# Causal scores in three blocks per head, spread over both column halves, no idle matmuls between the first round's digits, and one product more per digit in the second round

## The chip, the cores and the metric

One core of a Trainium2 chip. The metric is the time of one execution on the device in microseconds (us). The fast executions of one kernel in a group of runs agree within some 1.5%, so ratios are given with a 95% interval, from fast executions alone. Executions count as "slow" over 1.5% above the fastest of the same kernel. All others are undisturbed ("fast"). Engines are named as in the profile: PE (TensorE, matmul), PEld (its weight loads), DVE (VectorE), ACT (ScalarE), POOL (GpSimd), SP (SyncE, which issues most loads).

## The reference

Two parts, one after the other, with q, k, v and f_logit of 4 x 8 heads x 768 x 48 in fp32:

```python
f = sigmoid(f_logit)
for t in range(768):                                # gated linear attention, per head
    state = f[t][:, None] * state + outer(k[t], v[t])
    y[t] = q[t] @ state
x = y as (3072 tokens, 384)
logits = x @ w_gate                                 # 8 experts
# all 3072*8 logits in falling order; a token takes an expert that has fewer than 384 tokens
out[tokens of e] = relu(x[tokens of e] @ w1[e]) @ w2[e]      # 384 -> 1024 -> 384
```

## The kernel before

The attention runs in 24 chunks of 128 positions (6 for each of the 4 batches, all 8 heads at once). Each loop step works on several chunks at different stages: the pair of a part and a number is the part and how many steps the chunk lags. In the traces an engine's instructions run in the order of the program (ACT in one step: "high" at 93.84 us, the copies of x at 94.24, of q at 95.18, the decays from 96.86), so a part's place in this list is its place in an engine's queue.

```python
BANKS = {"bank": 6, "sum": 2}            # PSUM: six banks used in turn, two for the output sums

def scores(G):                            # A = k q^T, two keys halves j, two head parities par
    A = [ps("A") for _ in range(2)]
    ...
    for hp in range(HP):                  # HP = 4 head pairs
        for j in range(2):
            for par in range(2):
                ...                       # rows: the partitions of head 2*hp + par
                nc.tensor.matmul(out=A[par][HC*j:HC*j+HC, 128*hp:128*hp+128],     # HC = 64
                                 lhsT=G["kT"][rows, hp, HC*j:HC*j+HC],
                                 rhs=G["qT"][rows, hp, :], start=True, stop=True)
    for par in range(2):                  # the causal mask is applied in the copy out of PSUM
        nc.vector.copy_predicated(am[:, par], mask..., A[par]...)

FIRST = ((decayed, 2), (q_columns, 2), (k_columns, 2), (transposed, 5), (sums, 1))
FILLING = FIRST + ((x_copy, 5), (factors, 1), (k_copy, 2), (added, 2), (values, 4), (halves, 1),
                   (gate, 5), ..., (split, 0), (clamp, -1), (queries, 4), (scores, 3))
```

In the profile's lines A is the scores, T the transposes of q and k, X the transposes of x and the gate products, L the gate's cumulated sums, dS (part `added`) the state product, Y the outputs (`values`, then `queries`). ACT copies T to qT, Y to x, and prepares the decays.

After it come eight rounds of expert assignment. A round finds a threshold by digits (compare on DVE, count on PE), lists the tokens of an expert, gathers their rows by an indirect DMA from POOL, transposes them (Xe, copied to xeT by ACT) and runs the two expert products H and O. The products of one expert are queued one by one in `pe_work` and dealt out between the digits of the next round, so that PE has something to do:

```python
pace = {0: None, 1: (2, 1)}               # second round: 2 products before a count, 1 after it
for rnd in range(E - 1):
    slots, more = pace.get(rnd, (3, 2)), 3 if rnd > 1 else 0
...
pieces, last = ffn(L), []
if len(pe_work) >= 12:                    # hold two O products back to lie between the transposes
    last = [pe_work.pop() for _ in range(2)][::-1]
pe_work.extend(pieces[:TE] + last + pieces[TE:])        # pieces[:TE]: the three transposes Xe
```

In the first round there is no expert to deal out, and `idle_turns(n)` issues matmuls without a use; they are meant to keep PE's clock up (in the profiled execution it was 0.50 for 10.24 us in spite of them).

## Time and profile before

| before | |
|---|---|
| time, median of the first three runs | 470.13 us (468.16 to 470.71) |
| span of the profiled execution | 469.6 us |
| first output product Y starts | 21.59 us |
| last logits | 152.29 us |
| first expert's H starts | 180.46 us |
| period of the middle rounds, from H to H | 35.12 us |

These marks cut the span into parts that can be compared between kernels: start, 24 attention steps, first round, later rounds. The waits of PE's matmuls between 40 and 140 us (engine, line, what was waited for: us in total, times, longest):

```profile
PE A L308 <- ACT high L190: 1.0, 1, 1.0
PE X L352 <- ACT x L344: 0.8, 1, 0.8
PE A L308 <- issue: 0.6, 1, 0.6
PE Y L337 <- issue: 0.3, 1, 0.3
```

"issue" is standing still with nothing to wait for that the profile shows: 0.9 us here. And PE's timeline at the head of the third round (start, us, engine, line, operation, out<-in, shapes, count):

```profile
244.13 0.75 PE L944 MATMUL tokens<-number,in_line 128*128 128x6 bf16 x24
244.74 5.41 PE L1013 MATMUL O<-w,hT 128*128 128x384 f32 x16
...
250.07 1.54 PE L1013 MATMUL O<-w,hT 128*128 128x384 f32 x4
...
252.20 0.82 PE L991 MATMUL Xe<-ident,xe 128*128 128x128 f32 x6
```

Between the token list and the transposes lie 16 + 4 + 2 O records (the two records at 251.50 are not shown), 2 + 2 more follow between the transposes and the next H: 26 in all. While PE works on them, the gathers land: in the middle rounds the rows of one, 128 of 384 fp32 values, have come 2.7 us after its start on POOL (packets of q0 in the packed trace). The O records are a reserve, which covers this latency.

### The profile page before, as it was taken

The numbers are of one execution on the slowest core, as the hardware profiler recorded it, in microseconds if no ns is written. First come the engines' busy times: TensorE is split into PE (matmuls) and PEld (weight loads), VectorE is DVE, ScalarE is ACT, GpSimd is POOL, SyncE is SP. The second block draws the span as 40 slices with busy tenths as digits, with TensorE's granted clock in tenths as the row PEclk, the third lists the DMA queues.
The fourth block names the chain that finished last, engine by engine and source line by source line (L and its number), as shares of the span: only waits on it lengthen the run. The fifth ranks groups of instructions, "written<-read, shape, count | busy, mean of one in ns | idle before, by whom it ended". The sixth has DMA issues, their size and how long they took to land.

```text
span 469.6 us, 11983 instructions
## 1 busy us (share of the span) xinstructions
PE 445.2 (95%) x4910; PEld 298.9 (64%) x4910; DVE 263.1 (56%) x890; ACT 138.6 (30%) x322; POOL 131.8 (28%) x190
## 2 busy tenths in 40 slices
PE   8999999999999987899999999999999999999991
PEld 4788989899888444465565565565565565556550
DVE  5788867778896557736636636636646645000000
ACT  4666646566651002112212212212212212202200
POOL 2556635565540030023023023023023026001010
PEclk9999989999999689999999999999999999999997
DMA  8999988788211045082082072072082088300010
GB/s 168 203 194 212 208 180 184 164 180 189 70 52 55 2 159 162 0 286 81 4 287 82 4 285 83 2 285 86 0 285 85 0 287 272 133 18 34 0 37 21
DMA packets 118401, 59.14 MB, mean 126 GB/s; under 512 B 101664, under 2 KB 112960, under 8 KB 118336
## 3 DMA queue, kind: packets, MB, share of 16 engines
q1 hardware_dynamic: 111760, 44.06, 35.8%
q0 software_dynamic: 3072, 9.44, 6.2%
q10 hardware_dynamic: 3504, 4.77, 2.8%
q8 instruction: 41, 0.67, 0.6%
q14 instruction: 24, 0.20, 0.1%
HBM read 48.77 MB, written 9.49 MB: 124 GB/s over the span
## 4 chain that ended last, share of the span: by engine, by line
PE 68%; issue 14%; DVE 10%; POOL 3%; ACT 2%; DMA 1%; POOLq 0%; DVEq 0%; ACTq 0%
PE O L1013 19%; PE H L1002 16%; PE Y L323 5%; PE nothing L127 4%; PE A L308 4%; PE T L255 4%; PE Y L337 2%; PE dS L285 2%; PE X L352 2%; PE X L226 2%; PE L L201 2%; PE X L365 2%; POOL out_dram L1018 1%; DVE above L527 1%; DVE fillsb L520 1%
## 5 line engine op out<-in xcount | busy, mean ns | idle before, releaser
L1002 PE MATMUL H<-xeT,w 128*128 128x384 f32 x384 | 133.3, 495 | 0.6 <-ACT xeT L994 0.6
L1013 PE MATMUL O<-w,hT 128*128 128x384 f32 x384 | 131.4, 492 | 0.7 <-DVE beyond L527 0.7
L1013 PEld LDWEIGHTS O<-w,hT 128*128 128x128 f32 x384 | 70.1, 190 | 47.3 <-issue 5.9
L1002 PEld LDWEIGHTS H<-xeT,w 128*128 128x128 f32 x384 | 69.3, 190 | 45.6 <-issue 6.3
L1006 ACT ACTIVATE hT<-H 128x384 f32<-128x384 f32 x64 | 31.4, 491 | 105.4 <-PE H L1002 105.4
L1018 POOL DMA_INDIRECT out_dram<-o,token x24 | 24.2, 1010 | 107.5 <-ACT o L1017 105.4
L313 DVE COPY_PREDICATED am<-mask,A 128x512 f32<-128x512 int32 x48 | 32.5, 732 | 14.6 <-PE A L308 14.6
L1017 ACT COPY o<-O 128x384 f32<-128x384 f32 x24 | 11.5, 479 | 92.3 <-PE O L1013 91.6
L917 POOL TENSOR_TENSOR block<-past 128x72 f32<-128x72 f32 x8 | 2.4, 303 | 124.3 <-DVE at L527 108.6
L237 POOL TENSOR_TENSOR kg<-k,ek 128x384 f32<-128x384 f32 x23 | 23.1, 1005 | 48.8 <-ACT ek L215 48.8
L127 PE MATMUL nothing<-idle,ones 128*128 128x384 bf16 x133 | 31.6, 380 | 1.5 <-DVE ones L132 1.5
L959 POOL DMA_INDIRECT xe<-xd,token x24 | 23.3, 972 | 17.9 <-DVE used L524 10.8
L994 ACT COPY xeT<-Xe 128x384 f32<-128x384 f32 x24 | 10.7, 482 | 58.7 <-PE Xe L991 58.7
L308 PE MATMUL A<-qT,kT 48*64 48x128 f32 x768 | 26.1, 272 | 1.5 <-ACT high L190 1.0
L323 PE MATMUL Y<-v,am 128*64 128x48 f32 x768 | 27.0, 223 | 0.3 <-DVE am L313 0.3
L323 PEld LDWEIGHTS Y<-v,am 128*64 128x64 f32 x768 | 24.6, 138 | 1.4 <-DVE am L313 0.8
L191 POOL TENSOR_TENSOR low<-g,upper 128x384 fp32r<-128x384 f32 x22 | 22.2, 1009 | 7.2 <-DVE upper L188 5.5
L308 PEld LDWEIGHTS A<-qT,kT 48*64 48x64 f32 x768 | 21.0, 133 | 2.0 <-ACT high L190 1.1
L214 ACT ACTIVATE eq<-dl 128x384 f32<-128x384 f32 x24 | 12.6, 524 | 27.1 <-DVE dl L212 27.1
L127 PEld LDWEIGHTS <-ones 128*128 128x128 bf16 x133 | 12.9, 108 | 10.9 <-issue 4.7
L263 ACT COPY qT<-T 128x512 f32<-128x512 f32 x24 | 14.1, 587 | 11.9 <-PE T L255 8.9
L520 DVE TENSOR_TENSOR in_line<-line,counts 128x1024 bf16<-128x1024 bf16 x24 | 17.1, 765 | 0.3
(206 smaller groups left out, 614.6 us busy)
## 6 DMA issues: line engine op xcount, KB each, us to landing
w<-in_moe_w_dram SPq DMA_DIRECT2D x16, 1536.0 KB, 8.7
f<-in_f_logit_dram SPq DMA_DIRECT2D x24, 192.0 KB, 3.9
q<-in_q_dram SPq DMA_DIRECT2D x24, 192.0 KB, 3.8
k<-in_k_dram SPq DMA_DIRECT2D x24, 192.0 KB, 4.6
v<-in_v_dram SPq DMA_DIRECT2D x24, 192.0 KB, 3.8
xd<-x ACTq DMA_DIRECT2D x24, 192.0 KB, 3.3
xe<-xd,token POOLq DMA_INDIRECT x24
out_dram<-o,token POOLq DMA_INDIRECT x24
```

The costliest lines, as they stand in the source:

```text
L127: nc.tensor.matmul(out=nothing[:, 0:CAP], lhsT=ones[:], rhs=idle[:], start=True, stop=True)
L191: nc.gpsimd.tensor_tensor(out=low[:], in0=g[:, :, 0:DH], in1=upper[:].bitcast(FP32), op=ALU.subtract)
L237: engine.tensor_tensor(out=G["kg"][:, :, 0:DH], in0=G["k"][:], in1=G["ek"][:], op=ALU.mult)
L308: nc.tensor.matmul(out=A[par][HC * j:HC * j + HC, 128 * hp:128 * hp + 128], lhsT=G["kT"][rows, hp, HC * j:HC * j + HC], rhs=G["qT"][rows, ...
L313: nc.vector.copy_predicated(am[:, par], mask[:].unsqueeze(1).to_broadcast((128, HP, 128)), A[par][:].rearrange("s (a t) -> s a t", t=128))
L323: nc.tensor.matmul(out=Y[par][HC * j:HC * j + HC, DH * hp:DH * hp + DH], lhsT=G["am"][:, par, hp, HC * j:HC * j + HC], rhs=G["v"][:, 2 * h ...
L520: nc.vector.tensor_tensor(out=out_, in0=a, in1=b, op=op)
L959: nc.gpsimd.indirect_dma_start(out=xe[:], out_offset=None, in_=xd[:, :], in_offset=bass.IndirectOffsetOnAxis(ap=token[:, i:i + 1], axis=0))
L1002: nc.tensor.matmul(out=L["H"][:, 0:CAP], lhsT=L["w1"][:, d, 128 * ft:128 * ft + 128], rhs=xT[:, d, :], start=(d == 0), stop=(d == DC - 1))
L1006: nc.scalar.activation(out=hT[:, ft, :], in_=L["H"][:, 0:CAP], func=AF.Relu)
L1013: nc.tensor.matmul(out=L["O"][:, 0:D], lhsT=hT[:, ft, 128 * i:128 * i + 128], rhs=L["w2"][:, ft, :], start=(ft == 0), stop=(ft == FC - 1))
L1018: nc.gpsimd.indirect_dma_start(out=outs[next(tiles)][:, :], out_offset=bass.IndirectOffsetOnAxis(ap=L["token"][:, i:i + 1], axis=0), in_=o ...
```

## The change

Its intent: the upper triangle of a causal score block is zero, and the one of its four 64 x 64 blocks that lies wholly in it needs no matmul. Only three blocks per head are computed; for half of the head pairs one block goes to the other column half, so that both halves of the array get equal work. The output product then needs half of v on the other partitions, which ACT copies (`beside`). The never written blocks of A have to stay zero, so A gets two banks of its own. Besides, idle matmuls between the first round's digits go, with fewer in two longer fillers, and the second round deals out one product more per digit.

```diff
-    BANKS = {"bank": 6, "sum": 2}
+    BANKS = {"bank": 4, "sum": 2, "A0": 1, "A1": 1}
...
+    def more_constants():                 # on DVE, after attention step 3: mask of 512 columns,
+        ...                               # zero halves of vs, zero blocks of A
...
-        for hp in range(HP):
-            for j in range(2):            # 16 matmuls, all of 128 queries
+        blocks = [(hp, low, low, slice(0, C)) for hp in range(SW)]           # SW = 2
+        blocks += [(hp, high, high, high) for hp in range(SW, HP)]
+        blocks += [(hp, high, high, high) for hp in range(SW)]
+        blocks += [(hp, low, low, high) for hp in range(SW, HP)]
+        blocks += [(hp, high, low, low) for hp in range(SW, HP)]             # 20 matmuls
...
+    def beside(G):
+        G["vs"] = v_bufs[G["i"] % NB]
+        nc.scalar.copy(out=G["vs"][64:128], in_=G["v"][0:64, 2 * SW:H])
...
-                        (split, 0), (clamp, -1), (queries, 4), (scores, 3)))
+                        (split, 0), (clamp, -1), (beside, 3), (queries, 4), (scores, 3)))
...
-            idle_turns(2, bank("nothing", "O"))            # between the first round's digits
-            idle_turns(5 if last else 3, bank("nothing", "O"))
-                    idle_turns(26, bank("nothing", "O"))
+                    idle_turns(20, bank("nothing", "O"))
...
-                pe_work.extend(pieces[:TE] + last + pieces[TE:])
+                pe_work.extend(pieces[:TE - 1] + last[:1] + pieces[TE - 1:TE] + last[1:] + pieces[TE:])
...
-            pace = {0: None, 1: (2, 1)}
+            pace = {0: None, 1: (2, 2)}
...
+                some(pe_work, len(pe_work) // 2)           # before the last branch's load
```

Idle matmuls at the end of the attention go as well (not shown).

More of the change, by code (lines that the diff above doesn't have):

```diff
@@ L113 @@
     make_identity(nc, ident[:])
-    mask = kept([128, 128], I32, "mask")
+    SW = HP // 2
+    mask = kept([128, HP, 128], I32, "mask")
     ind = kept([128, 2], FP32, "ind")
@@ L122 @@
     a_bufs = [kept([128, 2, HP, 128], FP32, f"am{i}") for i in range(NB)]
+    v_bufs = [kept([128, H // 2, DH], FP32, f"vs{i}") for i in range(NB)]
+    A = [ps(f"A{par}", f"A{par}") for par in range(2)]
     def idle_turns(n, nothing):
@@ L132, in constants @@
         nc.vector.memset(ones[:], 1.0)
-        nc.vector.tensor_copy(out=mask[:], in_=wcum[:])
         nc.vector.tensor_scalar(out=wcum[0:64, :], in0=wcum[0:64, :],
@@ L151, in constants @@
         nc.vector.memset(zeros[:], 0.0)
+    def more_constants():
+        for rows, more in ((slice(0, 64), 1.0), (slice(64, 128), 0.0)):
+            nc.vector.tensor_scalar(out=mask[rows], scalar1=more, scalar2=None, op0=ALU.add,
+                                    in0=wcum[rows].unsqueeze(1).to_broadcast((64, HP, 128)))
+        nc.vector.memset(mask[0:64, SW:HP, 0:64], 0)
+        nc.vector.tensor_copy(
+            out=mask[64:128, SW:HP, 0:64],
+            in_=wcum[64:128].unsqueeze(1)[:, :, 64:128].to_broadcast((64, HP - SW, 64)))
+        for t in v_bufs:
+            nc.vector.memset(t[0:64], 0.0)
+        for par in range(2):
+            blocks = A[par][:].rearrange("s (a t) -> s a t", t=128)
+            nc.vector.memset(blocks[64:128, 0:SW, 0:64], 0.0)
+            nc.vector.memset(blocks[0:64, SW:HP, 0:64], 0.0)
     wg = const([128, DC, E], FP32, "wg")
@@ L302, in scores @@
         am = a_bufs[G["i"] % NB]
-        A = [ps("A") for _ in range(2)]
-        for hp in range(HP):
-            for j in range(2):
-                for par in range(2):
-                    rows = slice(DP * par, DP * par + DH)
-                    nc.tensor.matmul(
-                        out=A[par][HC * j:HC * j + HC, 128 * hp:128 * hp + 128],
-                        lhsT=G["kT"][rows, hp, HC * j:HC * j + HC],
-                        rhs=G["qT"][rows, hp, :], start=True, stop=True)
+        low, high = slice(0, HC), slice(HC, C)
+        blocks = [(hp, low, low, slice(0, C)) for hp in range(SW)]
[3 more added lines that the diff above has]
+        blocks += [(hp, high, low, low) for hp in range(SW, HP)]
+        for hp, place, keys, queries in sorted(blocks, key=lambda b: b[0] % SW):
+            for par in range(2):
+                rows = slice(DP * par, DP * par + DH)
+                nc.tensor.matmul(
+                    out=A[par][place, 128 * hp + queries.start:128 * hp + queries.stop],
+                    lhsT=G["kT"][rows, hp, keys], rhs=G["qT"][rows, hp, queries],
+                    start=True, stop=True)
         for par in range(2):
-            nc.vector.copy_predicated(
-                am[:, par], mask[:].unsqueeze(1).to_broadcast((128, HP, 128)),
-                A[par][:].rearrange("s (a t) -> s a t", t=128))
+            nc.vector.copy_predicated(am[:, par], mask[:],
+                                      A[par][:].rearrange("s (a t) -> s a t", t=128))
         G["am"] = am
+    def beside(G):
+        G["vs"] = v_bufs[G["i"] % NB]
+        nc.scalar.copy(out=G["vs"][64:128], in_=G["v"][0:64, 2 * SW:H])
     def values(G):
@@ L325, in values @@
                         lhsT=G["am"][:, par, hp, HC * j:HC * j + HC],
-                        rhs=G["v"][:, 2 * hp + par, :],
+                        rhs=(G["vs"][:, 2 * (hp - SW) + par, :] if j == 0 and hp >= SW else
+                             G["v"][:, 2 * hp + par, :]),
                         start=(hp == 0), stop=False, skip_group_check=True)
@@ L366, in gate @@
                                  start=(d == 0), stop=(d == DC - 1))
-    def warm(G):
-        if G["i"] == len(chunks) - 1:
-            idle_turns(4, ps("nothing", "sum"))
     def to_logits(G, to=None):
@@ L389 @@
                         (new_state, 2), (decays, 0), (gated_k, 1), (span, 1), (to_logits, 5),
-                        (split, 0), (clamp, -1), (queries, 4), (scores, 3)))
-    LAST = ((scores, 3),) + FIRST + ((x_copy, 5), (k_copy, 2), (values, 4), (queries, 4),
-                                     (warm, 5), (gate, 5), (to_logits, 5))
+                        (split, 0), (clamp, -1), (beside, 3), (queries, 4), (scores, 3)))
+    LAST = ((scores, 3), (beside, 3)) + FIRST + ((x_copy, 5), (k_copy, 2), (values, 4), (queries, 4),
+                                     (gate, 5), (to_logits, 5))
     small, small_pe = deque(), deque()
@@ L420 @@
     attention(2, 3)
-    nc.vector.memset(a_bufs[2][:], 0.0)
+    more_constants()
+    small.append(partial(nc.vector.memset, a_bufs[2][:], 0.0))
     nc.scalar.dma_start(out=xd[N:N + 32, :], in_=zeros[:])
@@ L712, in reached, with digit_alone @@
                 stt(above[:, c0:c1], over, digit, steps, op, ALU.is_ge)
-        def digit_alone(above, parts, choice, unit, last):
+        def digit_alone(above, parts, choice, unit):
             r = bank("cnt", "r")
@@ L784, in search @@
                 else:
-                    new, op_new = digit_alone(above, parts, choice, unit, size is digits[-1][2])
+                    new, op_new = digit_alone(above, parts, choice, unit)
                     over = less(over, digit, op)
@@ L1064, in assign_and_run @@
                     elif len(dve_work) > 1:
-                        idle_turns(3 if len(dve_work) > 4 else 1, bank("nothing", "O"))
+                        idle_turns(1, bank("nothing", "O"))
                 if rnd == 0:
-                    idle_turns(26, bank("nothing", "O"))
+                    idle_turns(20, bank("nothing", "O"))
                     for _ in range(TE - 1):
@@ L1107 @@
     assert not small
-    idle_turns(6, ps("nothing", "sum"))
     for piece in part(NCH - 1, NCH):
```

## The prediction

> **What bounds the kernel now.** I read the windows view first (one row for each stretch: start:end and length, then busy us of PE, PEld, DVE, ACT, POOL, then the granted clock, DMA share, GB/s).
>
> ```profile
> 100.00:120.00 20.00, 20.00 (x533) 18.37 (x535) 17.16 (x46) 12.57 (x33) 11.00 (x19) 1.00 0.86 189
> 156.63:166.87 10.24, 10.24 (x100) 4.52 (x99) 5.76 (x27) 0.00 (x0) 0.00 (x0) 0.50 0.01 2
> 180.00:200.00 20.00, 17.20 (x66) 8.44 (x67) 14.47 (x60) 3.35 (x7) 0.00 (x0) 1.00 0.12 45
> 200.00:300.00 100.00, 98.80 (x438) 57.75 (x437) 58.67 (x226) 19.14 (x40) 21.68 (x24) 1.00 0.38 131
> ```
>
> So there are four stretches with different limits. In the attention (to about 150 us) PE is busy 20.00 of 20.00. In the first round's digits (153 to 166 us) PE is "busy" only because of idle matmuls, at half the clock, and DVE works 5.76 of 10.24 us: a chain DVE, PE, DVE, PE. In the second round (180 to 197 us) PE has holes (17.20 of 20). After that PE is the bound again (98.8%). A gain counts if it shortens PE's own row in the first and the last stretch, or the DVE/PE chain in the two between.
>
> One attention step in the chain of waits (start, us, what):
>
> ```profile
> 99.05 0.89 PE A L308 x32
> 99.94 1.02 PE T L255 x8
> 100.96 0.33 PE X L352 x3
> 101.29 0.35 PE L L201 x2
> 101.64 0.60 PE dS L285 x16
> 102.24 0.93 PE Y L323 x32
> 103.18 0.43 PE X L226 x16
> 103.60 0.36 PE X L365 x12
> 103.96 0.61 PE Y L337 x32
> ```
>
> The pieces add up to 5.52 us and are all PE: nothing waits. The scores (A) cost 0.89 us a step, 24 steps.
>
> [...] Y L323 has 32 records on two column halves in 0.93 us, 16 for each half, 58 ns each, with 48 streamed columns; X L226 with 2 streamed columns takes 0.43/8 = 54 ns. [...] A has 32 records on four tiles, 8 each, 0.89/8 = 111 ns[...] (single records start 109 ns apart on a tile, and 7 ns apart on neighbouring tiles). [...] half clock from 64.47 for 3.41 us after a PE hole at 62 to 63 us, and from 156.63 for 10.24 us, three windows, in spite of the idle matmuls.
>
> **The change part by part.**
>
> 1. *Scores.* The zero block (early queries, late keys) is no longer computed. Before, each tile did 4 x 128 columns: 8 records of 109 ns = 0.87 us. Now a low tile has 2 of 128 and 2 of 64 columns (4 x 109 + 4 x 58 = 0.67 us), a high tile 6 of 64 (12 x 58 = 0.70 us[...]). So A goes from 0.89 to about 0.72, and the drain before T by 0.05 at most. ACT gets a copy of half of v each step (some 0.22 us of ACT time, from L344's two copies in 0.53 us) ahead of the two copies of x that X L352 waits for. In the timeline of the step at 93 us the second copy of x ends at 94.77 and X starts at 95.28: the slack of 0.5 is eaten by the copy (0.22) and by the earlier PE (0.15 to 0.2), just. I count 0.15 us for the 18 steps after about 50 us and 0.3 for the tail: -3.0. The banks (4 for the rest, two fixed for A) cost nothing: five allocations a step, each one's reader long done.
>
> 2. *Start.* The larger mask, the zeroed v copies and A's zeros are made on DVE at about 15 us: two tensor_scalars of 512 elements (0.4 to 0.6 each), nine small ones of 0.15 to 0.23, about 2.9 us where 0.91 us (the memset of am) stood; that memset follows one step later. So the next "upper" comes some 2 us later, with it "low" and L; PE has about 0.2 us to spare: +1.8. [...] at 60%, +1.0. In steps 5 to 8 X L352 already waits for x (0.45 and 0.34 us at 25.6 and 31.2), so there the copy of v adds: +0.5.
>
> 3. *First round's digits.* One digit at half clock (start, us, engine, line):
>
> ```profile
> 158.88 0.82 PE L127 MATMUL nothing<-idle,ones 128*128 128x384 bf16 x2
> 158.98 0.15 DVE L520 TENSOR_TENSOR fills<-cnt,wanted 16x8 f32<-16x8 f32 x1 [0.87 <-PE cnt L720]
> 159.17 0.15 DVE L530 TENSOR_REDUCE filled<-fills 16x1 bf16<-16x8 f32 x1
> ...
> 159.63 0.18 PE L728 MATMUL cnt<-filled,unit 16*128 16x1 bf16 x1
> ...
> 159.75 1.14 PE L127 MATMUL nothing<-idle,ones 128*128 128x384 bf16 x3
> ...
> 160.82 0.75 PE L720 MATMUL cnt<-choice,above 128*16 128x8 bf16 x24
> ```
>
> "filled" is ready at 159.32 and L728 starts at 159.63, behind two idle matmuls of 0.32; "above" is ready in thirds from 160.2 and the counts start at 160.82, behind three of them. The idle matmuls meant to keep the clock up delay the chain instead. Without: 0.25 and 0.4 us less for each of the three slow digits (2.63 to 1.97 us), 0.15 for the others, 0.25 before "sums": -2.3. The clock stays low through this stretch, which DVE hardly notices; the 20 idle matmuls before the gathers run at 0.32 at first, end within about 6 us of their start, and the gathered rows come 5 us after it: 0 to +0.5. The idle matmuls at the end of the attention lie behind waits for DVE: 0.
>
> 4. *Second round.* One expert matmul more for each of five digits. It moves 5 x 0.656 = 3.3 us of PE work into holes; a digit goes from 3.05 to about 3.3 us because the second count now waits 0.25 for PE: -1.7 to -2.0.
>
> 5. *Round boundaries.* That takes away the reserve. In the built order of the changed kernel the sequence at the head of each later round is: 8 O, count, six Xe, count, three Xe, H; before it was 8 O, count, 2 O, count, O, six Xe, count, three Xe, O, count, O, H. The O that covered the waits are gone. What then shows:
>
> ```profile
> 208.04 1.05 POOL L1018 DMA_INDIRECT out_dram<-o,token  x1 [3.41 <-ACT o L1017]
> ...
> 210.43 0.98 POOL L959 DMA_INDIRECT xe<-xd,token  x1 [1.34 <-DVE used L524]
> ...
> 212.97 0.95 POOL L959 DMA_INDIRECT xe<-xd,token  x1 [0.30 <-issue]
> ...
> 218.28 0.53 PE L991 MATMUL Xe<-ident,xe 128*128 128x128 f32 x3
> ...
> 218.84 0.48 ACT L994 COPY xeT<-Xe 128x384 f32<-128x384 f32 x1 [0.37 <-PE Xe L991]
> ...
> 220.13 1.45 PE L1002 MATMUL H<-xeT,w 128*128 128x384 f32 x4
> ```
>
> H needs the third xeT: 0.56 + 0.48 + 0.05 = 1.09 us after the third Xe starts, 0.33 of it PE work, so 0.7 us of hole that O's covered. The count's own DVE chain leaves 0.35. And the output of an O tile now finishes right before "tokens", so its scatter goes ahead of the gathers on POOL (+0.8 us); with 2.7 us from issue to landing (the packets of that queue) the third Xe waits another 0.7. Together 1.7 us of hole for 0.5 before: +1.2 for each of rounds 2 to 6, +6.0, with some chance of a window at half clock: +1.5.
>
> 6. *End.* The same hole at the last boundary but one, +1.8, and half the work put before the branch's load of "beyond" hides PE's 0.75 us wait there with its 0.1 restart: -0.9.
>
> Sum: -3.0 + 1.8 + 1.0 + 0.5 - 2.3 - 1.8 + 6.0 + 1.5 + 0.9 = +4.6, so 474.7. The boundary term is the largest and rests on latencies that I added by hand; someone who tuned such details will have looked at the time, which speaks against so large a loss. I shade to 472.5.
>
> **The rivals.** (a) The boundaries are covered (the gathers land early, or POOL's scatter doesn't go first): then rounds stay at 35.1 us each, the rest gives 467. For: in the old order DVE and POOL were early. Against: the O's are plainly not there in the order. (b) Tiles don't overlap with unequal columns: if the records run in lock step, A stays at 0.89 or becomes longer (5 steps of four records each half, 0.90): attention +3, in all 477. Against: 7 ns between the starts on four tiles. (c) The clock: holes of 1.7 us in a 3.4 us window at each boundary halve it each time: +1.7 x 6 in place of 1.5, 481. Against: windows at 167 and 177 us with PE half idle kept full clock. (d) PE's holes such as that at 62 us (about 2.7 us with its slow window) fall otherwise: 2 us either way.
>
> **Range and chances.** 472.5 us, 464 to 479.5 in 8 of 10: rival (a) with luck at the low end, (c) at the high end. Faster by over 2% (below 460.7) would need (a), no loss at the start and more than the whole of A's gain: 0.06. Slower by over 2% (above 479.5): (b) or (c): 0.12. Within: 0.82.
>
> **What would show it.** A in the chain at 0.70 to 0.75 and the step at 5.35; if not, 1 is wrong. "upper" of the fourth chunk near 21.3 in place of 19.03: 2. Digits at 1.97 us apart by "above": 3. L1002 to L754 without a hole in the second round: 4. From one round's "sums" to the next 36.3 in place of 35.12 us, with PE idle before Xe for a DMA and before H for ACT xeT: 5. If rounds stay at 35.1, the prediction is too high by 6 us.

## The result, and the profile after

The changed kernel takes 491.8 us (median of 4 runs, 491.37 to 495.14). The kernel before took 469.14 us in the same rounds. The ratio is 1.050, 95% interval 1.044 to 1.056: slower, and outside the predicted range. Ratios are the mean time of one kernel's fast runs over that of the other's of the same rounds, so not quite the ratio of the medians that are quoted.

The marks show where the 20.7 us between the two profiled executions (469.6 and 490.3) come from. (By the clock it is 22.7 us between medians: the profiled execution of the kernel before was slower than most.)

| stretch | before, us | after, us | difference |
|---|---|---|---|
| start to first Y | 21.59 | 24.15 | +2.6 |
| first Y to last logits | 130.70 | 139.07 | +8.4 |
| last logits to first H | 28.17 | 25.73 | -2.4 |
| first H to the end | 289.1 | 301.3 | +12.2 |

**Start.** DVE's timeline; the last line is the step that the next chunk's chain waits for, which started at 16.51 us before:

```profile
14.94 1.57 DVE L160 TENSOR_SCALAR mask<-wcum 64x512 int32<-64x512 f32 x2
...
18.56 0.17 DVE L172 MEMSET A<- 64x128 f32 x1
18.64 0.53 DVE L233 TENSOR_SCALAR dl<-L 128x384 f32<-128x384 f32 x1
```

**Attention steps.** The chain of waits around one step (start, us, what):

```profile
93.42 0.49 issue
93.91 0.35 ACT vs L344
...
94.28 0.55 ACT x L373 x2
94.85 0.34 ACTq L376
...
95.23 0.59 ACT qT L284
...
95.87 0.67 PE dS L306 x16
96.55 0.93 PE Y L351 x32
...
98.26 0.61 PE Y L366 x32
```

Before, every piece of such a step was PE. Now a stretch from 93.91 to 95.87 us is ACT: the copy of v, the copies of x, issuing x's store, the copy of q. PE works on T, X and L in this stretch, but dS, which is next, can begin only when q is copied: its weight load waited 0.42 us for qT. In the 24 steps this pattern comes and goes. The scores themselves did get shorter: whole ones in this chain take 0.71 us instead of 0.89. Yet the median of the 13 steps in the middle (from dS to dS) went from 5.52 to 6.17 us, and the shortest of them from 5.52 to 5.61. PE's waits in the same window as above:

```profile
PE A L333 <- issue: 2.3, 5, 0.7
PE X L381 <- ACT x L373: 1.8, 4, 0.7
PE T L276 <- issue: 1.3, 1, 1.3
PE Y L366 <- issue: 1.2, 2, 0.7
```

Standing still without a named cause grew from 0.9 to 5.2 us (with two groups of 0.2 not shown). These stalls sit in dense parts of PE's instruction stream, half of them in the scores, and each follows a packet of 16384 bytes on the "instruction" DMA queue q8. That queue has 41 packets before, 42 after. Two of the experiments below change PE's instructions alone: with 1536 more q8 has six packets more, with 768 fewer three fewer, 256 to a packet both times. At that count the 4910 matmuls and 4910 weight loads before make 38.4 packets, so q8 seems to carry PE's own instructions, at 16384/256 = 64 bytes each (an estimate from these counts). The packets' times, read from the packed trace, are telling: they lie 3.6 to 6.4 us apart between 40 and 140 us, and each of the ten stalls of the changed kernel ends 1.33 to 1.50 us after the end of one. The same holds for every stall without a named cause in that window of all 19 traces: 82 of them, all of which end 1.16 to 1.69 us after a packet's end (of 64 waits with a named cause, 22 do). So I read these stalls as waits for PE's next instructions; that is inferred from these times and counts.

**Round boundary.** PE's timeline at the head of the third round, at which the kernel before had 26 O records:

```profile
257.55 0.75 PE L968 MATMUL tokens<-number,in_line 128*128 128x6 bf16 x24
258.16 5.41 PE L1037 MATMUL O<-w,hT 128*128 128x384 f32 x16
...
264.33 0.55 PE L1015 MATMUL Xe<-ident,xe 128*128 128x128 f32 x3 [0.32 <-DMA xe<-xd,token]
...
265.85 0.55 PE L1015 MATMUL Xe<-ident,xe 128*128 128x128 f32 x3 [0.92 <-DMA xe<-xd,token]
266.96 1.56 PE L1026 MATMUL H<-xeT,w 128*128 128x384 f32 x4 [0.57 <-ACT xeT L1018]
```

In brackets stands how long the engine was idle before, and what ended it. 16 O records are left of 26, and 0.32 + 0.92 + 0.57 = 1.81 us of PE lie open. The periods from H to H are 39.3, 38.7, 37.0, 37.0, 38.7, 36.9, 32.8 us; before they were 39.67, four of 35.12, 36.11, 31.95. The two of 38.7 have another cause on top (windows view; columns as in the prediction):

```profile
225.19:228.60 3.41, 1.69 (x10) 0.98 (x9) 2.24 (x9) 1.67 (x4) 1.09 (x1) 1.00 0.37 119
228.60:232.01 3.41, 3.41 (x9) 1.82 (x8) 0.78 (x3) 0.00 (x0) 0.00 (x0) 0.50 0.00 0
```

After 3.41 us in which PE was busy for 1.69 (1.60 the second time), the granted clock is 0.50 for 3.41 us (I call such a stretch a window; the longer stretches at half clock in the two profiles, up to PE's last product, are 10.24 and 20.48 us, three and six of it). It happens twice, at 228.60 and 341.24 us; the first four H take 2.62 and 2.71 us there, 1.56 in the third round. Half of such a window, 1.7 us, is my estimate of what it loses. Busy time in the profile does not tell where half clock follows: 2.18 of 3.41 us (from 262.73 us) was followed by full clock, and in the kernel before 2.43 (from 61.06 us) by 0.50.

### The profile page after: what moved, and what is told of

It is laid out like the page before. It is cut to its first block, busy times and chain, and to the rows that moved or that the text cites.

```text
span 490.3 us, 12301 instructions
## 1 busy us (share of the span) xinstructions
PE 441.6 (90%) x5051; PEld 295.5 (60%) x5051; DVE 263.6 (54%) x900; ACT 149.6 (31%) x346; POOL 131.4 (27%) x190
## 4 chain that ended last, share of the span: by engine, by line
PE 43%; issue 31%; DVE 9%; POOL 7%; ACT 5%; DMA 3%; ACTq 1%; POOLq 0%; DVEq 0%
PE H L1026 12%; PE O L1037 9%; PE Y L351 4%; DMA xe<-xd,token 3%; POOL xe L983 3%; POOL out_dram L1042 2%; PE dS L306 2%; PE A L333 2%; PE T L276 2%; PE nothing L133 2%; PE X L247 2%; PE X L394 2%; PE Y L366 2%; ACT x L373 1%; ACT qT L284 1%
## 5 line engine op out<-in xcount | busy, mean ns | idle before, releaser
L1026 PE MATMUL H<-xeT,w 128*128 128x384 f32 x384 | 138.5, 508 | 4.0 <-ACT xeT L1018 4.0
L1037 PE MATMUL O<-w,hT 128*128 128x384 f32 x384 | 127.9, 489 | 0.0
L1037 PEld LDWEIGHTS O<-w,hT 128*128 128x128 f32 x384 | 71.8, 190 | 48.9 <-issue 2.0
L983 POOL DMA_INDIRECT xe<-xd,token x24 | 25.1, 1048 | 11.4 <-issue 4.9
L333 PE MATMUL A<-qT,kT 48*64 48x64 f32 (+1 forms) x960 | 24.7, 232 | 3.7 <-issue 2.6
L133 PE MATMUL nothing<-idle,ones 128*128 128x384 bf16 x82 | 21.1, 411 | 1.5 <-DVE ones L138 1.5
L235 ACT ACTIVATE eq<-dl 128x384 f32<-128x384 f32 x24 | 12.6, 524 | 25.7 <-DVE dl L233 25.7
L546 DVE TENSOR_TENSOR own<-cnt,mine 128x64 f32<-128x64 f32 x30 | 6.7, 224 | 22.4 <-PE cnt L763 22.4
L1015 PE MATMUL Xe<-ident,xe 128*128 128x128 f32 x72 | 12.5, 285 | 7.0 <-DMA xe<-xd,token 7.0
L546 DVE TENSOR_TENSOR fillsb<-cnt,wanted 128x128 f32<-128x128 f32 x30 | 8.7, 292 | 18.1 <-PE cnt L778 18.1
L387 DVE COPY xT<-X 128x384 f32<-128x384 f32 x24 | 13.3, 556 | 9.0 <-PE X L381 8.3
```

Of the source, the lines that this page charges most:

```text
L133: nc.tensor.matmul(out=nothing[:, 0:CAP], lhsT=ones[:], rhs=idle[:], start=True, stop=True)
L333: nc.tensor.matmul(out=A[par][place, 128 * hp + queries.start:128 * hp + queries.stop], lhsT=G["kT"][rows, hp, keys], rhs=G["qT"][rows, hp ...
L546: nc.vector.tensor_tensor(out=out_, in0=a, in1=b, op=op)
L983: nc.gpsimd.indirect_dma_start(out=xe[:], out_offset=None, in_=xd[:, :], in_offset=bass.IndirectOffsetOnAxis(ap=token[:, i:i + 1], axis=0))
L1026: nc.tensor.matmul(out=L["H"][:, 0:CAP], lhsT=L["w1"][:, d, 128 * ft:128 * ft + 128], rhs=xT[:, d, :], start=(d == 0), stop=(d == DC - 1))
L1037: nc.tensor.matmul(out=L["O"][:, 0:D], lhsT=hT[:, ft, 128 * i:128 * i + 128], rhs=L["w2"][:, ft, :], start=(ft == 0), stop=(ft == FC - 1))
```

## The experiments

Sixteen kernels and a seventeenth were run, each with the kernel before in the same rounds. Medians of those comparison runs lay between 469.7 and 471.9 us.

| kernel | median us | ratio to before, 95% interval |
|---|---|---|
| attention only | 482.44 | 1.030 (1.024 to 1.036) |
| rounds only | 482.6 | 1.031 (1.025 to 1.037) |
| attention, v by DMA | 486.74 | 1.034 (1.027 to 1.042) |
| attention, v copied after q | 476.34 | 1.016 (1.011 to 1.021) |
| before, scores in halves | 484.18 | 1.028 (1.022 to 1.034) |
| before, with the copy of v | 475.54 | 1.010 (1.003 to 1.016) |
| before, with the fixed banks | 471.69 | 1.000 (0.994 to 1.006) |
| before, with copy and banks | 478.89 | 1.017 (1.008 to 1.026) |
| digits only | 468.82 | 0.997 (0.992 to 1.002) |
| pace only | 483.49 | 1.026 (1.021 to 1.031) |
| attention, no copy | 477.58 | 1.016 (1.010 to 1.022) |
| attention, constants earlier | 482.51 | 1.022 (1.015 to 1.028) |
| pace, repaid in the third round | 472.15 | 1.007 (1.002 to 1.013) |
| changed kernel, pace undone | 478.82 | 1.018 (1.010 to 1.025) |
| before, scores twice as wide | 468.71 | 0.999 (0.994 to 1.004) |
| changed attention mended, and digits | 472.08 | 1.004 (0.999 to 1.010) |
| attention, state product later | 482.82 | 1.029 (1.021 to 1.037) |

### The change in two halves

Attention only: the changed kernel with every edit behind the attention undone, the warming matmuls at its end staying out. Rounds only: the kernel before with the digits' edit, the pace and the half of `pe_work` before the branch; the order of pieces stayed as before.

> The change's attention (scores of three blocks, copy of v, fixed banks, larger constants) with the rounds of the kernel before. The last copy of logits comes at 163.2 us in the changed kernel and at 152.3 in the one before. Theory (attention and rounds are separate losses): +10.9 us, so about 480, with the rounds 35.1 us apart as before. Rival (the attention's loss is an effect of something else, such as the code's length): below 475.

> The attention of the kernel before with the changed rounds (no idle matmuls between the digits, two expert matmuls in the second slot of the second round, half of the work ahead of the branch). Theory: digits -2.4 us, second round +1.4, boundaries about +1.9 each and a window at half clock at one or two of them, in all +7 to +10: 477 to 480. Rival (the slow windows come from the later start only): +3 to +5.

Each half alone costs about 13 us (482.44 and 482.6 against 469.69), so each has a loss of its own. Together that is 25.7 us, 3 more than the changed kernel lost. The next section finds about as much: a loss in the first round's digits that the attention alone has, and the changed kernel doesn't.

### Rounds: digits, pace, and the debt

```diff
# digits only, on the kernel before
-            idle_turns(2, bank("nothing", "O"))
-            idle_turns(5 if last else 3, bank("nothing", "O"))
-                        idle_turns(3 if len(dve_work) > 4 else 1, bank("nothing", "O"))
+                        idle_turns(1, bank("nothing", "O"))
-                    idle_turns(26, bank("nothing", "O"))
+                    idle_turns(20, bank("nothing", "O"))
# pace only, on the kernel before
-            pace = {0: None, 1: (2, 1)}
+            pace = {0: None, 1: (2, 2)}
```

> The kernel before, with only the idle matmuls between the first round's digits taken out (and the longer fillers cut to what the changed kernel has); attention and pace as before. The prediction's step for the digits was -2.3 us; the changed kernel's trace shows the digits' intervals at 1.92 us instead of 2.6. If that stands by itself the time falls by 2 to 2.5 us, to about 467, and the verdict is same. If the clock falls to half in the first round for longer [...], the saving is lost: 469 to 472.

> The kernel before with the second round's pace alone changed, (2, 1) to (2, 2): O matmuls are used up one more per digit in the second round. Theory 'reserve spent': each later boundary between two rounds then stands open for 1.9 us while the gather and the transposed copy land, with periods of 37.0 us instead of 35.12, five or six times, against 1.4 gained or lost in the second round: +8 to +12 us, 478-482. Rival 'order of pieces or clock': the pace alone moves under 2 us and the boundaries stay at 35.12.

The profile seems to show the gain that was expected: 24.8 us from the last logits to the first H, where the profiled execution before had 28.2. But that one had half clock over its digits. The windows view from the first digit's second matmul to the last digit's, of that execution and of the trace of "pace, repaid" (below), which has the same first round:

```profile
155.00:164.89 9.89, 9.89 (x121) 4.54 (x120) 5.37 (x24) 0.00 (x0) 0.00 (x0) 0.58 0.01 2
153.63:161.31 7.68, 7.68 (x121) 4.42 (x120) 5.28 (x24) 0.00 (x0) 0.00 (x0) 1.00 0.01 2
```

At full clock four digits take 7.68 us with the idle matmuls in place, 1.92 each, and that is what they take without. Only at half clock do the idle matmuls cost 0.7 us a digit (2.63). Six traces with this first round and no half clock in it (pace only, pace repaid, scores in halves and twice as wide, with the copy of v, with copy and banks) need 25.5 to 26.2 us from the last logits to the first H. So the edit gained 0.7 to 1.4 us there, and by the clock the ratio is 0.997, with an interval that includes no change.

This concerns the attention too. All six kernels with the changed attention and the old rounds have 13.7 to 30.7 us of half clock around the last logits, 2.60 to 2.63 us a digit, and 27.9 to 28.8 us to the first H: about 2 to 3 us that are counted as the attention's cost, but lost in the digits. The changed kernel has the half clock as well (20.48 us from 163.75 us), and without idle matmuls loses nothing by it (25.7). Those six also lack the warming matmuls at the attention's end, and wait for a bank in its tail. Whether either has to do with the fall of the clock was not tested: no run puts the warming matmuls back.

The pace alone, one number, costs 11.6 us between medians. Its periods from H to H are 39.4, 37.0, 37.1, 38.7, 37.1, 36.9, 33.4: the changed kernel's periods, with a half clock window (at 291.38 us) in the one of 38.7. So neither the order of pieces nor the missing idle matmuls makes the open boundaries.

One product more per digit in the second round only: why do later rounds suffer? The idea is a debt. Each later round adds one expert's products to the queue and takes as many out; what the second round takes too much (five products, one in each of five digits: the ten O records that are gone) is missing at every boundary thereafter. Then paying it back once must close them:

```diff
-            pace = {0: None, 1: (2, 1)}
+            pace = {0: None, 1: (2, 2), 2: (3, 1)}
```

> The kernel before with pace (2, 2) in the second round and (3, 1) in the third, so the third gives back the O matmuls that the second spent. Theory 'carried deficit': one boundary, the second to the third round, stands open (+1.9 us), all later periods are 35.12 us; the time is 1 to 4 us over before, 472-475, not 12 over. Rival 'the pace itself or the clock': periods stay near 37.0 us and the time near 483.

The periods are 39.4, 37.01, 35.13, 35.11, 35.12, 36.11, 31.94, and no half clock window falls between the first H and PE's last product. The time is 472.15 us, ratio 1.007 where the pace alone has 1.026. PE's timeline at the heads of the second and the third expert's products:

```profile
214.67 0.55 PE L991 MATMUL Xe<-ident,xe 128*128 128x128 f32 x3 [0.71 <-DMA xe<-xd,token]
215.78 0.91 PE L1002 MATMUL H<-xeT,w 128*128 128x384 f32 x2 [0.57 <-ACT xeT L994]
...
249.73 0.82 PE L991 MATMUL Xe<-ident,xe 128*128 128x128 f32 x6
```

One boundary is open, the next has its 26 O records again and is closed. The 37.01 is not what I had expected it to be: the open boundary lies before the second H, in the first period, where the gain in the second round hides it. The 1.9 us of the second period are the price of paying back: with one product fewer a digit of the third round takes 3.24 us instead of 3.50, though a product is 0.656, so PE loses 0.4 us to waits for DVE in each of five digits. This settles the mechanism: the third round, with the same products and the same engines, closes what the second opened.

```diff
# on the changed kernel, nothing else
-            pace = {0: None, 1: (2, 2)}
+            pace = {0: None, 1: (2, 1)}
```

> The changed kernel with only the pace of the second round put back to (2, 1). Theory 'carried deficit': periods of 35.12 us again, no half clock windows in the later rounds, time down by 10 to 13 us, to 479-482. If the other order of the pieces, which the change also has, were part of the loss, holes would remain at the boundaries and less than 8 us would come back.

The time is 478.82 us (four runs, one of them slow at 484.91; the fast ones 476.2 to 479.56, median 478.08), 13.7 us under the changed kernel by the fast ones, with four periods of 35.14 to 35.16 us. The new order of pieces, which is in there, costs at most 0.04 us a period there.

### Attention: banks, copy, or both

```diff
# copy of v, on the kernel before (its result is read by nobody)
+    v_bufs = [kept([128, H // 2, DH], FP32, f"vs{i}") for i in range(NB)]
+    def beside(G):
+        G["vs"] = v_bufs[G["i"] % NB]
+        nc.scalar.copy(out=G["vs"][64:128], in_=G["v"][0:64, H // 2:H])
-                        (split, 0), (clamp, -1), (queries, 4), (scores, 3)))
+                        (split, 0), (clamp, -1), (beside, 3), (queries, 4), (scores, 3)))
# fixed banks, on the kernel before
-    BANKS = {"bank": 6, "sum": 2}
+    BANKS = {"bank": 4, "sum": 2, "A0": 1, "A1": 1}
```

> The kernel before, plus the ScalarE copy of half of v in the place of the program where the kernel after has it; its result is read by nobody. Banks, scores, rounds unchanged. Theory 'copy in front of x and q': the 0.35 us stands in front of the x and q copies in each step, undisturbed steps go from 5.4 to about 5.7 and the time rises by 4 to 7 us, 474-477. Rival 'instruction supply': the copy is off the path, +0 to +1.5 us. Rival 'banks': six rotating banks give the copy slack, so alone it costs +0 to +2 us and the waits of the tensor engine's state product for the q copy stay near zero.

> The kernel before with the banks of the kernel after: four rotating, two fixed for the scores, two for the sums. No copy. The tail of the attention should show the second of two back to back scores waiting for the masked copy of the first, +1.3 us; the rest of the attention has no late copy to wait for, so +0 to +0.5 there: 470.5-472. If the banks alone cost 4 us or more, the bank accounting of the prediction is the failed step.

> The kernel before with both the unread copy of v and the banks of the kernel after; scores as before. Theory 'copy in front of x and q, with the state product on the q product's bank': more than the sum of copy alone and banks alone; undisturbed steps 5.9 to 6.1, the time 476-480. Theory 'instruction supply': tail of +1.3 and little else, 471-473.

Banks alone: nothing that the clock can see. The copy alone: 3.7 us between medians, in the profile +0.5 in each of four early steps (5.88 against 5.38, on average) and +0.1 in the undisturbed ones in the middle (5.62 against 5.52). Both: 7.1 us, early steps of 6.0. The intervals of copy and of copy with banks overlap, so that the banks make the copy worse is suggested and not shown.

The reverse was done on the changed attention: the copy left out (`values` reads v in its place, so the result is wrong), the copy put elsewhere, and the copy made by a DMA.

```diff
# no copy
-                        rhs=(G["vs"][:, 2 * (hp - SW) + par, :] if j == 0 and hp >= SW else
-                             G["v"][:, 2 * hp + par, :]),
+                        rhs=G["v"][:, 2 * hp + par, :],
-                        (split, 0), (clamp, -1), (beside, 3), (queries, 4), (scores, 3)))
+                        (split, 0), (clamp, -1), (queries, 4), (scores, 3)))
# copied after q: beside moves behind q_columns, one stage later
-    FIRST = ((decayed, 2), (q_columns, 2), (k_columns, 2), (transposed, 5), (sums, 1))
+    FIRST = ((decayed, 2), (q_columns, 2), (beside, 4), (k_columns, 2), (transposed, 5), (sums, 1))
# by DMA
-        nc.scalar.copy(out=G["vs"][64:128], in_=G["v"][0:64, 2 * SW:H])
+        nc.sync.dma_start(out=G["vs"][64:128], in_=G["v"][0:64, 2 * SW:H])
```

> The changed attention (scores of three blocks, its banks, masks and constants) with the rounds of the kernel before, and without the copy of v: the early rows of the upper half use v where it stands, so the result is wrong on purpose. What remains of the attention's +12 to +14 us is what scores, start and tail cost without the copy. Copy with banks cost 7.9 us on the kernel before: so 474 to 475.5 is expected, with 2.0 to 2.5 us of it the start, 1.3 the tail, and no wait of the state product for the q copy. If stalls without a named releaser were the larger part, it stays at 477 or more. If it falls to 471 or less, the copy is the whole loss.

> As the attention alone, but ACT copies v right after qT, in a hole of its own (about 1.1 us before eq), not between high and x. Theory 1: as with the DMA, 470 to 474. Theory 2: 475 to 478. If ACT's time as such were the trouble and not its place, no gain: 480.

> As the attention alone, but half of v is copied across by a DMA from SBUF to SBUF and not by ACT. Theory 1 (ACT's copy of 0.35 us sits in front of x and qT, and X, dS wait for them): the waits of X for x and of dS for qT go, step near 5.4, time 470 to 473. Theory 2 (TensorE's instruction fetch stalls, about one a step, come from the faster A and the extra instructions): stalls of 0.5 to 0.9 us stay, 475 to 478. Theory 3 (the start's DVE work and the banks): 478 or more.

Without the copy the attention's cost falls from 1.030 to 1.016; with the copy behind the q copy it is 1.016 as well. From the first Y to the last logits the traces have 132.2 us in both, 138.2 in the attention alone. So it is not ACT's 0.35 us of work that costs these 1.4% (6.6 us), but the place: ahead of x and q. In both kernels undisturbed steps are 5.35 us, the very figure predicted. The DMA also gives steps of 5.34 to 5.36, but three stretches at half clock (6.8, 3.4 and 27.3 us) and one step of 10.46 us as well, and no time is gained. The trace names PE's longest wait: at 24.65 us Y stands 3.0 us for this very DMA (the copy is issued on SP behind three loads), and the first of the half clock stretches follows. The rest was not followed up.

I then held a narrower theory. In the chain shown above, the four ACT pieces end in qT and release dS, because with only four rotating banks dS takes the bank that T leaves when qT is copied; the chain closes over Y, the gate and the next copy in 5.62 us, which is the undisturbed step of every kernel that has the copy there. If so, doing Y before dS on PE opens the loop:

```diff
-                        (added, 2), (values, 4), (halves, 1), (gate, 5), (gated_q, 1),
+                        (values, 4), (added, 2), (halves, 1), (gate, 5), (gated_q, 1),
```

> The changed attention with the rounds of the kernel before; the copy of v stays where it is, but the tensor engine does the output product before the state product, so that the state product's wait for the q copy (whose bank it takes) has 0.93 us more. Theory 'closed loop through ScalarE': the loop of 5.62 us is opened, undisturbed steps go to 5.35-5.5 us and the time falls from 482.4 to 476-479. Rival 'the copy delays x, whatever the state product does': steps stay at 5.6 or more and the time at 481-484. If the later state lengthens another chain, steps stay long for that reason, and the chain of waits will name it.

This theory fell. The waits of dS for qT are gone from the trace, and yet the time is 482.82 us and undisturbed steps are 5.61 to 5.63 us. The chain of waits now goes another way from the copy:

```profile
84.30 0.35 ACT vs L344
...
84.67 0.55 ACT x L373 x2
...
85.26 0.56 PE X L381 x3
```

and from there over DVE's xT and dl, ACT's decays, POOL's kg, and the next step's "high" to the next copy. As far as these chains show, several loops of nearly equal length pass through ACT ahead of x; the copy lengthens all of them, and opening one leaves the others. That is read from two chains, and not shown by a run.

### Attention: the start

```diff
     constants()
+    more_constants()                      # mask, 1.9 us, into DVE's idle stretch at 6.0 us
     ...
     attention(0, 2)
+    yet_more_constants()                  # vs and A zeros, into that at 10.2 us
     attention(2, 3)
-    more_constants()
```

> The changed attention with the rounds of the kernel before, its 3.7 us of new constants on VectorE moved from the start's chain into two idle stretches of VectorE seen in the trace (1.9 us each, at 6.0 and 10.2 us). The first output product should start 2 us earlier (22.2 instead of 24.2-24.5 us from the start) and the time fall from 482.4 by 2 us to 480-481. If the constants were not on the path, no change.

The first Y starts at 22.37 us in the profile (24.45 in the attention alone), as expected. By the clock the ratio goes from 1.030 to 1.022, with intervals that overlap, and medians hardly differ; the profiled execution had 34 us at half clock. The 2.1 us are shown by the trace alone.

### Attention: standing still without a cause

The attention without the copy has 0.17 us shorter steps when undisturbed, and still costs 7 us. About 2.9 are the start, and 2.0 to 2.7 the digits at half clock (28.2 us from the last logits to the first H against 25.5 to 26.2, see above). Of the rest the trace says: first Y to last logits takes 132.2 us, against 130.7 in the profile before and 129.2 to 131.6 in the four other traces with that attention, though twenty steps of 0.17 should have saved 3. The issue waits are 4.6 us in the same 100 us. Over all traces they are 0.8 to 3.0 us in eight kernels with 16 score matmuls a step, and 2.5 to 5.2 in ten with 20 or 32. Is it the rate at which PE's instructions must be supplied? Two kernels change nothing but that: the kernel before with each score matmul of 128 queries cut into two of 64, or two joined into one of 256 (with the first pair's keys, so a wrong result).

```diff
# in halves
+                    for z in range(0, 128, 64):
                         nc.tensor.matmul(
-                            out=A[par][HC*j:HC*j+HC, 128*hp:128*hp+128], lhsT=...,
-                            rhs=G["qT"][rows, hp, :], start=True, stop=True)
+                            out=A[par][HC*j:HC*j+HC, 128*hp+z:128*hp+z+64], lhsT=...,
+                            rhs=G["qT"][rows, hp, z:z+64], start=True, stop=True)
# twice as wide
-        for hp in range(HP):
+        for hp in range(0, HP, 2):
-                            out=A[par][HC*j:HC*j+HC, 128*hp:128*hp+128],
-                            rhs=G["qT"][rows, hp, :], ...
+                            out=A[par][HC*j:HC*j+HC, 128*hp:128*hp+256],
+                            rhs=G["qT"][rows, hp:hp+2, :].rearrange("p h t -> p (h t)"), ...
```

> The kernel before, each score matmul of 128 queries issued as two of 64: same blocks, same banks, same results, no copy of v, but twice the instructions in about the same tensor time, so the densest part of the instruction stream is denser than in the kernel after. Theory 'instruction supply' (the kernel after loses in the middle of the attention because its short score matmuls run faster than instructions arrive): score stalls that wait for nothing appear in the chain and the time rises by 3 to 6 us, to 473-476. Theory 'copy in front of x and q' (ScalarE's copy of v is what lengthens the steps): only the longer scores are seen, 0.05 us by 23 steps, about +1 us, 470-471.5.

> The kernel before with each pair of score matmuls of 128 queries issued as one of 256, with the keys of the first: the same tensor time with 8 instead of 16 matmuls in a step; the result is wrong on purpose. Theory 'instruction supply': stalls in the scores without a releaser shrink or go, undisturbed steps stay 5.4 to 5.5, and the time falls by 2 to 5 us, to 465-468. Rival: stalls have another cause, nothing changes beyond 1 us.

In halves, the kernel is 12.4 us slower between medians. Some of it is the matmuls' own time:

```profile
73.46 1.05 PE A L309 x61
```

1.05 us instead of 0.89 is 0.16 a step, 3.8 us in 24 steps. The rest is waiting: the issue waits are 4.6 us in the 100 us, the middle steps have a median of 6.36 us, and loads of k (3.2 and 3.6 us) come into the chain. q8 has 47 packets, six more than before, for 2 x 768 added instructions. With wide scores there are 38 packets (three fewer, for 2 x 384 instructions less), but issue waits of 1.5 us and the same time as before, against my expectation of 2 to 5 us. So a denser stream costs much here, and a thinner one gains nothing (1.5 us is within what the same attention has in other traces). What the stalls wait for is read from the packets' times above (82 of 82 end 1.16 to 1.69 us after one): the next packet of instructions. That the changed attention has more of them because its scores are denser (20 matmuls in 0.71 us instead of 16 in 0.89) is consistent with all of this. Why a packet comes too late, and how much of the attention's loss these waits make, stays open.

### The parts put together

The changed attention with the copy behind q and the constants in DVE's idle stretches, the digits' edit, and the old pace:

> The changed attention with the copy of v moved behind the q copy of the step before and the new constants in VectorE's idle stretches, no idle matmuls between the first round's digits, pace (2, 1). If the parts add up: 482.4 less 6 for the copy's place, less 2 to 4 for the constants, less 1.3 to 2.5 for the digits: 470 to 473, the same as before, since stalls and the wait at the tail eat what shorter scores save. If it is under 465 the change would have been worth keeping once mended.

472.08 us against 469.8, ratio 1.004 (0.999 to 1.010): the faults found are the whole loss within the noise, and shorter scores, mended, gain nothing that can be seen. None of the kernels is shown to beat the kernel before; the digits' edit alone (0.997) comes nearest.

## Why the prediction was wrong

Sum before shading: +4.6 us. Measured between the profiles: +20.7. By its own steps:

- **1, scores, -3.0: this step failed, by most of the miss.** A's cost was right (0.72 predicted, 0.71 measured; the 0.72 was an estimate from the trace's 109 ns for a record of 128 columns and 58 ns for one of 48, and that one of 64 would take 58 ns as well was assumed), and so was the step of 5.35 us, which kernels without the copy in that place reach. What failed is the sentence that the slack of 0.5 us would be eaten by the copy "just". The copy took 0.35 us, not 0.22, and stands in ACT's queue ahead of x and q, in loops that had no slack: 1.4% by the clock. The prediction scaled a pair of copies out of PSUM, 0.53 us; a single one of these, of 192 elements a partition like the copy of v, takes 0.30 to 0.33 us in the same trace, already more than 0.22. In place of -3.0 the 13 steps in the middle took 4.1 us more (0.1 to 0.7 us a step) and what follows them up to the last logits 2.0. The stalls of the denser stream were nowhere in the prediction. "The banks cost nothing" held by the clock when the banks alone were changed, but not in the tail, where two scores come back to back: before, their 64 records are one piece of 1.76 us in the chain; after, 1.34 us of the first's masked copy lie between them, since the second must wait for its fixed banks. The banks alone bring the same piece (1.32 us), and no time is seen for it.
- **2, start, +1.8 and +0.5: mechanism right, sizes low.** Measured +2.6 to the first Y. Steps 5 to 8 were to lose 0.5 us to the copy of v; the four early steps took 2.3 us more, and 0.3 more in the attention without the copy. The +1.0 was a chance of 60%, my estimate, times the 1.7 us that one window of 3.41 us at half clock was taken to cost, such as the profile before has at 64.47 us after a wait of 1.0 us; none came before 163.75 us.
- **3, first round's digits, -2.3: right by luck.** Between the profiles it is -2.4, with intervals of 1.92 us where 1.97 was predicted. But the term took the half clock of one execution for the kernel's usual state. At full clock the digits took 1.92 us before the change too, and the changed kernel's 25.7 us to the first H lie within the 25.5 to 26.2 of the six traces named above: no gain. It fits that the loss by the clock, 22.7, is larger than that between the profiles.
- **4, second round, -1.7 to -2.0: right.** From the first H to the second the changed kernel gained 0.4; with the open boundary in that period, 1.9, this is -2.3 and one boundary (by subtraction; no run has the one without the other).
- **5, round boundaries, +1.2 each: mechanism right, size wrong.** The holes are those that were named (gather, then xeT), and 1.81 us of them agree with the 1.7 predicted. The scatter does go ahead of the gathers: the first gather starts 2.28 us after the token list (257.55 us), 1.43 before (244.13), so 0.85 later where 0.8 was predicted. But 0.5 us was taken off for holes that the kernel before was said to have; its trace has 0.28 there, before a count, and the period grew by 1.9 (37.0 less 35.12), not by 1.2. Clock windows cost 2 x 1.7, by the estimate above, instead of 1.5.
- **6, end, +0.9: low**, +1.6 over the last two periods.
- **The shading** from 474.7 to 472.5, because a tuned change would hardly lose so much, went the wrong way.

Of the rivals none came true as named: the clock rival (c) had half clock after each boundary, and it came after two. The two windows held against it, at 166.87 and 177.11 us, had PE busy for 2.25 and 2.21 of 3.41 us at full clock.

## What to carry to other kernels

Work added to an engine that is 30% busy is not free when its instructions run in the order of the program, as here, and every step's result passes through it (0.35 us a step cost 6.6 us in the place it had, and none to be seen in another): ask what stands behind the new instruction, and put it after the pieces that others wait for. A queue of work that is dealt out to fill holes is a stock: taking more out at one place empties every later place until it is paid back, and paying back has its price (1.9 us here), so follow its length through all rounds. Fewer columns in more, shorter matmuls need not be a saving: here PE stood still without a named cause for 0.8 to 3.0 us in 100 with 16 score matmuls a step, for 2.5 to 5.2 with 20 or 32. Try the same work in more instructions to see what that costs (12.4 us here). And one profile is one execution: before a stretch of it becomes a term of a prediction, see by the granted clocks of other runs whether it is the usual one.
